# Score bursts in one tile size, another order of loads and other due times in an attention and feed-forward kernel

## The chip, the core and the metric

The kernel runs on one core of a Trainium2 chip. The core has five engines that run their own instruction streams side by side: TensorE (PE in the profile, with its weight loads shown apart as PEld), VectorE (DVE), ScalarE (ACT), GpSimd (POOL) and SyncE (SP). DMA transfers are issued here by POOL, which can convert fp32 to bf16 on the way, and by SP, which also issues the transfers that transpose. The metric is the device time of one execution in microseconds (us); lower is better.

## What is computed

A sliding-window attention with a distance bias, followed by a feed-forward layer with a squared ReLU:

```
q, k, v: [8 batches, 8 heads, 576 positions, 64]      # fp32
scores = (q @ k.T) / 8 + slope[h] * -(|i - j|)         # only for 0 <= i - j < 128
attn   = softmax(scores) @ v
x      = attn as [4608 tokens, 512]
h      = x @ w_in            # [4608, 2048]
out    = max(h, 0)**2 @ w_out  # [4608, 512], fp32
```

## The kernel before

**Blocks.** Each batch's 576 positions are cut into four blocks of 128 and one of 64, so there are 40 blocks, m = 0 to 39, five to a batch. A block's q and k are loaded into one tile of the ring `kq`, its v into one of the ring `vt` (eight and seven tiles; `size`, line 256). They arrive as bf16 through POOL's queue, but for block 0, whose k and q come as fp32 through SP into a tile of their own. A block takes these steps:

- `turn` (429) transposes k and q into a tile `kqT`: blocks 0 to 8 (`KQ_PE`) on PE, with the copies out of PSUM on ACT and DVE (414, 416); the others by a DMA transpose that SP issues (439). After it the `kq` tile is free.
- `score` (501) makes the scores in bursts of matmuls, then takes the exponential on ACT and multiplies by a table of decayed masks on DVE.
- `mix` (593) multiplies by v (609), normalises (632, 637), and transposes x into `xT`: on PE with a DVE copy for the blocks in `X_PE` (655, 414), by a DMA transpose for the others (647).

**Tiles in a burst.** A score matmul contracts over 64 numbers, so two heads lie in the two halves of the rows of the array. From block 6 on (`QUARTERS`) a block that has a left neighbour, and 128 rows, is done in *quarters*: matmuls of 64x64 tiles that leave out the part outside the window (513 to 523, tag `Pq`; L520 in the profile). All others, the *pairs* among them, use 64x128 tiles (524 to 531, tag `P`; L528). A pair is the short last block of a batch with the first of the next: (4,5), (9,10) and so on to (34,35), seven in all. Each block or pair is cut into two units of two head groups; up to pair (4,5) a burst has two units, from block 6 on three (`LONG`, `UNITS`). So a pair from (9,10) on shares bursts with quartered blocks. A pair has 24 matmuls: for each of four head groups, three pieces (64, 64 and 128 columns) in two halves.

**Feed-forward.** The 4,608 tokens form nine groups of 512. `fc_step` (713) makes 16 first-layer tiles a group, each of four matmuls, then ReLU on ACT and the square on DVE; `t_part` (775) sums the second layer over 16 tiles for each 128 tokens, in four parts, each with one quarter of `w_out`. Groups 0 and 1 are split by tokens (`SPLIT`), so that the first tiles need fewer blocks. The weights come in four loads each, i0 to i3 for `w_in` and o0 to o3 for `w_out`. PSUM's eight banks are shared by all of this.

**What sets the order.** Nothing is scheduled by hand. Each piece of work is added to a `Plan` (44) as a task with an engine, a cost in ns, a key, what it waits for and what buffers it takes and frees. `order` (90) simulates the engines: it starts, again and again, the task that can start first, and among those the one with the lowest key. The result is a fixed order of instructions for each engine; on the chip an instruction that has to wait holds up all behind it on its engine. What steers the planner:

- keys. The feed-forward's run from 0, 128 to a group (64 first-layer, 64 second-layer). A block's key is its due time from `where` (418): its last token's number / 4, less 232, less `AHEAD` for the block. Transposes by DMA take due - 80, those of k and q on PE due - 56, scores and masks due - 28, the rest due - 12 to due.
- loads. `FIRST` is the order of the first ten blocks (b) and the weights (i, o) on POOL's queue; they have keys below all others. Later blocks' loads are issued when a tile is free. The planner lets at most eight loads be open in a queue.
- `BEGIN`, POOL's assumed start; `COLD`, the time up to which PE's costs count double; `SHARE, SOON`, which hold back PSUM banks from the feed-forward when a score burst will be ready within `SOON` ns.
- `PAIR_AFTER`: the two DVE copies that build the pairs' masks (316, 319; key -140) wait for this block's masks.
- `WARM` and `FILL`: idle matmuls on a zero tile (815) at the start (four to an instruction), and in holes that the plan shows on PE before `UNTIL`; `fill` (827) puts in so many that they take the share `FILL` of the hole, at 107 ns each before `COLD` and 54 after.

At the end the number of transfers that SP issues is made to fit the eight DMA lanes: `odd` of the stores before the last four go through POOL (753).

Of the kernel before, what the change touches and what calls it, by code (L numbers as in the profile page):

```python
# [38 lines left out]
class Plan:  # L39


    LAT = {"PE": 260.0, "ACT": 220.0, "DVE": 220.0, "POOL": 200.0, "SP": 2200.0}
    BEGIN = {"POOL": 780.0}

    def __init__(self, bufs, pools, cold, share):
        self.tasks = []
# [31 lines left out]
    def order(self):  # L78
# [6 lines left out]
        for t in self.tasks:  # L85
# [3 lines left out]
            for e in t.engs:  # L89
                free.setdefault(e, self.BEGIN.get(e, 800.0))  # L90
                cand.setdefault(e, [])
# [105 lines left out]
def kernel(  # L197
    ctx: ExitStack, tc: tile.TileContext, q, k, v, moe_w_in, moe_w_out, out
):
    nc = tc.nc  # L200
# [10 lines left out]
    C = d_model // 128  # L211
# [1 line left out]
    NG = NT // 512  # L213
    NBLK = B * NKB

    FIRST = "b0 b1 b2 b3 i0 i1 i2 b4 b5 o0 b6 o1 b7 o2 i3 o3 b8 b9"
    SPLIT = {0: [(0, 256), (256, 512)], 1: [(0, 192), (192, 320), (320, 512)]}
    EARLY = 0
    AHEAD = {10: -30, 1: 30, 4: 90, 9: -60, 5: 30, 0: 0, 12: 60, 11: 0, 2: -60, 8: 0, 7: 90, 6: 0, 3: -30, 24: 0, 14: -30, 18: 30, 25: 30, 23: 30, 16: -30, 13: 30, 21: 0, 19: 30, 17: 0, 22: 0, 20: 60, 15: 30}
    LEAD = 40  # L220

    KQ_PE = [0, 1, 2, 3, 4, 5, 6, 7, 8]
    X_PE = [0, 1, 2, 3, 4, 5, 6, 7, 8, 12, 13, 17, 21]
    WARM = 24
    FILL, UNTIL = 0.7, 26e3
    COLD = 8200
    QUARTERS = 6
    V0 = 1
    SHARE, SOON = 3, 1500
    LONG, UNITS = 5, 3  # L230
    W_IN = [0, 4, 8, 12, 16]
    PAIR_AFTER, PAIR_KEY = 1, -140
    BANKS = {"A": 8}
    HOLD, OSB = 12, 14

# [17 lines left out]
        return [const.tile(shape, BF16, name=f"{name}_{i}") for i in range(n)]  # L253


    size = {"kq": 8, "v": 7, "kqT": 5, "P": 2, "x": 4, "Pq": 2, "raw": 2}
    kq = ring("kq", size["kq"], [128, 2, d_model])
    vt = ring("vt", size["v"], [128, H, D + 1])
    kqT = ring("kqT", size["kqT"], [128, 2 * C, 128])
    Pt = {nm: ring(nm, size[nm], [128, H, 2, 128]) for nm in ("P", "Pq")}  # L260
    raw = ring("raw", size["raw"], [128, H, 192])
# [5 lines left out]
    def act(n):  # L267
        return n * 0.84 + 55.0
# [133 lines left out]

    for i, what in enumerate(FIRST.split()):
        {"b": load_block, "i": load_w_in, "o": load_w_out}[what[0]](int(what[1:]), -9e5 + i)
# [13 lines left out]
    def where(m):  # L418
        b, kb = divmod(m, NKB)
        return b, kb, blk[kb], (b * S + kb * 128 + blk[kb]) / 4 - 192 - 40 - AHEAD.get(m, LEAD if m not in X_PE else 0), b == 0  # L420

# [79 lines left out]
    def score(units):  # L501
        first_of = [u for u in units if u[1] == 0]
        due = units[0][0][3]
        slots = {}
        for (ms, sP, work_of, _), j in units:
            for half in range(2):
                slots[ms[0], 2 * j + half] = Slot("A")

        def burst():
            for sl in slots.values():  # L510
                bank(sl)
            for (ms, sP, work_of, _), j in units:
                for c in (2 * j, 2 * j + 1) if sP.tag == "Pq" else ():
                    m = ms[0]
                    for part, k0, q0, q1 in ((1, 0, 0, 128), (1, 64, 64, 128), (0, 64, 0, 128), (0, 0, 0, 64)):
                        mk = m - 1 + part
                        lo = (c % 2) * 256 + at_of[m, part] + q0 - k0
                        for half in range(2):
                            rows = slice(half * 64, half * 64 + 64)
                            nc.tensor.matmul(  # L520
                                slots[m, 2 * j + half].tile[k0:k0 + 64, lo:lo + q1 - q0],
                                kqT[sk_of[mk].idx][rows, c, k0:k0 + 64], kqT[sk_of[m].idx][rows, C + c, q0:q1],
                                start=True, stop=True)
                for c in () if sP.tag == "Pq" else (2 * j, 2 * j + 1):
                    for m, mk, w, at, _ in work_of:
                        for half in range(2):
                            rows = slice(half * 64, half * 64 + 64)
                            nc.tensor.matmul(  # L528
                                slots[ms[0], 2 * j + half].tile.rearrange("p (c x) -> p c x", c=2)[:, c % 2, at:at + w],
                                kqT[sk_of[mk].idx][rows, c, :], kqT[sk_of[m].idx][rows, C + c, 0:w],  # L530
                                start=True, stop=True)
        cost = 220.0 + 2 * sum(88.0 if u[0][1].tag == "Pq" else sum(max(w[2], 64) / 2.4 + 4 for w in u[0][2])
                               for u in units)
        tm = plan.add({"PE": cost}, due - 28, burst,
                      [t for u in units for w in u[0][2] for x in w[:2] for t in t_kq_of[x]] + chain["s"],
                      [*slots.values()] + [u[0][1] for u in first_of if u[0][1].tag == "P"],
                      [x for u in units if u[1] == 1 for w in u[0][2] for x in w[4]])
        tm.n = 4 * sum(4 if u[0][1].tag == "Pq" else len(u[0][2]) for u in units)
        plan.bursts.append(tm)
        chain["s"] = [tm]  # L540
        for (ms, sP, work_of, due), j in units:
            pair = len(ms) == 2
            hi = max(w[3] for w in work_of) // 128 + 1
            lo = min(w[3] for w in work_of) // 128
            n = 128 if pair else work_of[0][2]
            cols = 2 * sum(w[2] for w in work_of)

            def view(t, pair=pair, lo=lo, hi=hi, n=n):
                if pair:
                    return t  # L550
                return t.rearrange("p c (t q) -> p c t q", t=2)[:, :, lo:hi, 0:n]

            for i in (2 * j, 2 * j + 1) if sP.tag == "Pq" else ():
                slot = slots[ms[0], i]
                if i == 0:
                    raw_of[ms[0]] = Slot("raw")
                sr = raw_of[ms[0]]

                def expo(i=i, slot=slot, sr=sr):
                    nc.scalar.activation(raw[sr.idx][:, 2 * i:2 * i + 2],  # L560
                                         slot.tile.rearrange("p (c x) -> p c x", c=2)[:, :, 0:192],
                                         AF.Exp, bias=0.0, scale=scale)
                te = plan.add({"ACT": act(384) + 50.0}, due - 28 + 3 * i, expo, [tm], [sr] if i == 0 else [], [slot])
                for k0 in (0, 64):
                    def mask(i=i, k0=k0, sr=sr, sP=sP):
                        nc.vector.tensor_tensor(  # L566
                            Pt["Pq"][sP.idx].rearrange("p h t q -> p h (t q)")[k0:k0 + 64, 2 * i:2 * i + 2, k0:k0 + 192],
                            raw[sr.idx][k0:k0 + 64, 2 * i:2 * i + 2],
                            masks.rearrange("p h t q -> p h (t q)")[k0:k0 + 64, 2 * i:2 * i + 2, k0:k0 + 192],
                            op=ALU.mult)  # L570
                    P_of[ms[0]][1].append(plan.add(
                        {"DVE": dve(384, 2)}, due - 28 + 3 * i, mask, [te] + t_zero_P + t_mask,
                        [sP] if i == 0 and k0 == 0 else [], [sr] if i == 3 and k0 else []))
            for i in () if sP.tag == "Pq" else (2 * j, 2 * j + 1):
                slot = slots[ms[0], i]

                def Pv(i=i, sP=sP, view=view):
                    return view(Pt["P"][sP.idx][:, 2 * i:2 * i + 2].rearrange("p h t q -> p h (t q)"))

                def expo(i=i, Pv=Pv, view=view, slot=slot):  # L580
                    nc.scalar.activation(Pv(i), view(slot.tile.rearrange("p (c x) -> p c x", c=2)),  # L581
                                         AF.Exp, bias=0.0, scale=scale)
                te = plan.add({"ACT": act(cols) + 50.0}, due - 28 + 3 * i, expo, [tm], [], [slot])

                def mask(i=i, pair=pair, Pv=Pv, view=view):
                    pt = Pv(i)
                    mk = (pair_masks if pair else masks.rearrange("p h t q -> p h (t q)"))[:, 2 * i:2 * i + 2]
                    nc.vector.tensor_tensor(pt, pt, view(mk), op=ALU.mult)  # L588
                P_of[ms[0]][1].append(plan.add(
                    {"DVE": dve(cols, 2)}, due - 28 + 3 * i, mask,  # L590
                    [te] + (t_pair if pair else [t_mask[h] for h in range(H) if place(h) // 2 == i])))
# [73 lines left out]
    sk_of, t_kq_of, parts_of, P_of, at_of = {}, {}, {}, {}, {}  # L665
    m = 0
    raw_of = {}
    units, ready = [], []
    while m < NBLK:
        ms = [m, m + 1] if m % NKB == NKB - 1 and m + 1 < NBLK else [m]  # L670
# [4 lines left out]
        for j in range(2):  # L675
# [6 lines left out]
            units = []  # L682
# [190 lines left out]
```

## Time and profile before

| | us |
|---|---|
| median of 5 runs | 314.63 (313.65 to 315.8) |
| the profiled execution | 315.8 |
| its span in the profile | 314.0 |
| PE busy | 299.0 |
| DVE busy | 184.7 |
| ACT busy | 171.2 |
| POOL busy | 106.1 |
| PE first-layer matmuls (L713) | 148.0 |
| PE second-layer matmuls (L775) | 142.4 |
| first L713 starts | 18.14 |
| last block load issued by POOL | 212.01 |

Times in views of the trace are counted from the start of the span; the rest of the execution's time lies around it. Matmuls follow each other in a pipeline, and the duration of one holds its latency, so durations of neighbours overlap, and a sum of them is more than the time that PE was taken. DMA rows of POOL and SP are the issuing of a transfer, not its landing. A group's line gives the count, the busy time and the mean of one in ns, then the engine's idle time before them.

### The profile page before, as it was taken

How to read it: one execution, taken by the hardware profiler on the slowest of the kernel's cores; microseconds unless marked ns; L12 is line 12 of the kernel's file. 1: busy time of each engine (PE TensorE's matmuls, PEld its weight loads, DVE VectorE, ACT ScalarE, POOL GpSimd, SP SyncE). 2: the span in 40 equal slices, each digit the busy share in tenths (PEclk: the TensorE clock that was granted, in tenths of full speed). 3: DMA queues.
4: the chain of work that ended last, by engine and by line, in shares of the span. 5: the costliest groups of instructions: out<-in, count | busy, mean ns of one | idle time of the engine just before them, and what ended most of it. 6: DMA issues, size and time to landing. Idle time of an engine off the chain costs nothing.

```text
span 314.0 us, 7547 instructions
## 1 busy us (share of the span) xinstructions
PE 299.0 (95%) x2955; PEld 167.9 (53%) x2998; DVE 184.7 (59%) x566; ACT 171.2 (55%) x338; POOL 106.1 (34%) x132
## 2 busy tenths in 40 slices
PE   7879999999989989999999999999999999999996
PEld 3567778767545555554545544554454544444443
DVE  7765677758469597885785853774587522222200
ACT  5867567566166774665665834673564543434411
POOL 8938639565354563474173220000000000000000
PEclk9999999999999999999999999999999999999999
DMA  9999999999999999999999999995312310000022
GB/s 134 150 185 174 189 185 122 141 150 134 134 132 141 155 138 133 145 130 141 128 195 154 203 143 179 257 144 132 111 41 71 111 43 35 33 34 35 33 88 79
DMA packets 167668, 39.76 MB, mean 127 GB/s; under 512 B 158864, under 2 KB 163216, under 8 KB 167632
## 3 DMA queue, kind: packets, MB, share of 16 engines
q0 software_dynamic: 114736, 18.36, 84.8%
q1 hardware_dynamic: 52896, 20.92, 41.3%
q8 instruction: 23, 0.38, 0.5%
q14 instruction: 13, 0.11, 0.1%
HBM read 36.70 MB, written 9.44 MB: 147 GB/s over the span
## 4 chain that ended last, share of the span: by engine, by line
PE 81%; DMA 8%; DVE 4%; POOL 4%; issue 2%; ACT 1%; POOLq 0%
PE A L713 36%; PE A L775 35%; PE A L609 5%; DMA kqT<-kq 4%; DMA kq<-in_q_dram 4%; PE A L520 3%; DVE Pq L566 2%; POOL kq L397 2%; PE A L528 1%; POOL vt L397 1%; PE A L655 1%; ACT raw L560 1%; PE A L467 1%; DVE x L637 1%; POOL w_in_sb L366 1%
## 5 line engine op out<-in xcount | busy, mean ns | idle before, releaser
L713 PE MATMUL A<-xT,w_in_sb 128*128 128x512 bf16 (+3 forms) x757 | 148.0, 325 | 3.1 <-DMA w_in_sb<-in_moe_w_in_dram 2.0
L775 PE MATMUL A<-w_out_sb,g 128*128 128x512 bf16 (+2 forms) x560 | 142.4, 373 | 2.6 <-issue 1.9
L722 ACT ACTIVATE rt<-A 128x512 bf16<-128x512 f32 (+1 forms) x148 | 86.5, 591 | 99.8 <-PE A L713 76.6
L729 DVE TENSOR_TENSOR g<-rt 128x512 bf16<-128x512 bf16 (+1 forms) x148 | 60.7, 412 | 75.0 <-ACT rt L722 74.2
L713 PEld LDWEIGHTS <-w_in_sb 128*128 128x128 bf16 x768 | 68.5, 98 | 53.4 <-DMA w_in_sb<-in_moe_w_in_dram 2.6
L775 PEld LDWEIGHTS <-g 128*128 128x128 bf16 x592 | 54.0, 98 | 54.3
L566 DVE TENSOR_TENSOR Pq<-raw,masks 64x384 bf16<-64x384 bf16 x168 | 59.1, 352 | 9.7 <-ACT raw L560 6.3
L397 POOL DMA_DIRECT2D vt<-in_v_dram x40 | 34.1, 854 | 53.6 <-PE A L609 33.7
L397 POOL DMA_DIRECT2D kq<-in_k_dram x39 | 33.6, 861 | 33.8 <-DMA kqT<-kq 17.1
L397 POOL DMA_DIRECT2D kq<-in_q_dram x39 | 33.5, 859 | 16.4 <-DMA kq<-in_q_dram 6.2
L560 ACT ACTIVATE raw<-A 128x384 bf16<-128x384 f32 x84 | 35.7, 501 | 4.3 <-PE A L520 3.8
L745 ACT ACTIVATE osb<-A 128x512 f32<-128x512 f32 (+1 forms) x36 | 21.5, 598 | 22.7 <-PE A L775 22.4
L637 DVE TENSOR_TENSOR x<-A,rec 128x256 bf16<-128x256 f32 (+1 forms) x80 | 31.8, 412 | 0.7
L753 POOL DMA_DIRECT2D out_dram<-osb x1 | 0.6, 587 | 85.5 <-ACT osb L745 85.5
L581 ACT ACTIVATE P<-A 128x512 bf16<-128x512 f32 (+1 forms) x48 | 23.7, 577 | 4.2 <-PE A L528 4.1
L632 DVE RECIPROCAL rec<-A 128x4 f32<-128x4 f32 (+1 forms) x80 | 12.8, 173 | 14.2 <-PE A L609 13.3
L609 PEld LDWEIGHTS <-Pq 128*128 128x128 bf16 x336 | 15.6, 97 | 10.0 <-DVE Pq L566 1.2
L609 PE MATMUL A<-vt,Pq 128*128 128x65 bf16 x336 | 17.4, 193 | 1.6 <-DVE x L637 0.9
L588 DVE TENSOR_TENSOR P<-P,pair_masks 128x512 bf16<-128x512 bf16 x28 | 11.6, 421 | 3.4 <-ACT P L581 2.6
L609 PEld LDWEIGHTS <-P 128*128 128x128 bf16 x240 | 10.8, 98 | 4.8
L609 PE MATMUL A<-vt,P 128*128 128x65 bf16 x240 | 11.8, 193 | 0.0
L520 PEld LDWEIGHTS <-kqT 64*64 64x64 bf16 x672 | 8.4, 108 | 6.0 <-issue 5.7
(43 smaller groups left out, 109.2 us busy)
## 6 DMA issues: line engine op xcount, KB each, us to landing
out_dram<-osb SPq DMA_DIRECT2D x34, 256.0 KB, 2.3
vt<-in_v_dram POOLq DMA_DIRECT2D x32, 128.0 KB, 10.2
kq<-in_k_dram POOLq DMA_DIRECT2D x31, 128.0 KB, 11.2
kq<-in_q_dram POOLq DMA_DIRECT2D x31, 128.0 KB, 11.0
w_in_sb<-in_moe_w_in_dram POOLq DMA_DIRECT2D x4, 512.0 KB, 11.6
w_out_sb<-in_moe_w_out_dram POOLq DMA_DIRECT2D x4, 512.0 KB, 9.9
kq<-in_k_dram POOLq DMA_DIRECT2D x8, 64.0 KB, 12.4
kq<-in_q_dram POOLq DMA_DIRECT2D x8, 64.0 KB, 12.2
```

What stands on the lines that cost most here:

```text
L397: nc.gpsimd.dma_start(o, src[b, :, kb * 128:kb * 128 + n, :].rearrange("h s d -> s h d"))
L520: nc.tensor.matmul(slots[m, 2 * j + half].tile[k0:k0 + 64, lo:lo + q1 - q0], kqT[sk_of[mk].idx][rows, c, k0:k0 + 64], kqT[sk_of[m].idx][ro ...
L560: nc.scalar.activation(raw[sr.idx][:, 2 * i:2 * i + 2], slot.tile.rearrange("p (c x) -> p c x", c=2)[:, :, 0:192], AF.Exp, bias=0.0, scale ...
L566: nc.vector.tensor_tensor(Pt["Pq"][sP.idx].rearrange("p h t q -> p h (t q)")[k0:k0 + 64, 2 * i:2 * i + 2, k0:k0 + 192], raw[sr.idx][k0:k0 ...
L581: nc.scalar.activation(Pv(i), view(slot.tile.rearrange("p (c x) -> p c x", c=2)), AF.Exp, bias=0.0, scale=scale)
L609: nc.tensor.matmul(bank(slot_v)[:, hi * (D + 1):(hi + 1) * (D + 1)], Pt[sP.tag][sP.idx][:, place(h)].rearrange("p t q -> p (t q)")[:, at_o ...
L637: nc.vector.tensor_tensor(xt[sx.idx][0:n, hf * 256:(hf + 1) * 256].rearrange("p (h e) -> p h e", h=4), pv[0:n, :, 0:D], srec.tile[0:n, :]. ...
L713: nc.tensor.matmul(bank(slot)[:, fi * w:(fi + 1) * w], w_in_sb[:, cc, fc * 128:(fc + 1) * 128], xT[:, cc, g * 512 + lo:g * 512 + hi], star ...
L722: nc.scalar.activation(srt.tile[:, 0:cols], slot.tile[:, 0:cols], AF.Relu, bias=0.0, scale=1.0)
L729: nc.vector.tensor_tensor(sg.tile[:, fcs[0]:fcs[-1] + 1, lo:hi], r, r, op=ALU.mult)
L745: nc.scalar.activation(so.tile[:, lo:hi], slot.tile[:, lo:hi], AF.Copy)
L775: nc.tensor.matmul(bank(slot)[:, lo:hi], sg.tile[:, fc, t * 128:(t + 1) * 128], w_out_sb[:, fc, lo:hi], start=fc == 0, stop=fc == FCB - 1)
```

## The change

In `score`, a burst that holds a quartered unit makes its other units with 64x64 tiles too: each of their matmuls, 128 columns of the array wide, becomes two of 64, one for each half of the keys. The columns that stream through are the same. Bursts without a quartered unit are as before.

In `FIRST` the quarters of the weights move: o0 ahead of b4, i3 and o1 ahead of b6, o2 behind b7, o3 between b8 and b9. In `AHEAD` six blocks get another value: 4 from 90 to 60, 5 from 30 to 60, 8 from 0 to -30, 3 from -30 to 30, 14 from -30 to 60, 13 from 30 to 90. Blocks 13 and 21 leave `X_PE`, so their x is transposed by DMA. The ring `kq` has seven tiles for eight. Five numbers of the planner and of the fillers change, and the pairs' masks are built after block 2 instead of block 1.

```diff
--- before.py
+++ after.py
@@ -40,7 +40,7 @@
 
 
     LAT = {"PE": 260.0, "ACT": 220.0, "DVE": 220.0, "POOL": 200.0, "SP": 2200.0}
-    BEGIN = {"POOL": 780.0}
+    BEGIN = {"POOL": 1260.0}
 
     def __init__(self, bufs, pools, cold, share):
         self.tasks = []
@@ -213,23 +213,23 @@
     NG = NT // 512
     NBLK = B * NKB
 
-    FIRST = "b0 b1 b2 b3 i0 i1 i2 b4 b5 o0 b6 o1 b7 o2 i3 o3 b8 b9"
+    FIRST = "b0 b1 b2 b3 i0 i1 i2 o0 b4 b5 i3 o1 b6 b7 o2 b8 o3 b9"
     SPLIT = {0: [(0, 256), (256, 512)], 1: [(0, 192), (192, 320), (320, 512)]}
     EARLY = 0
-    AHEAD = {10: -30, 1: 30, 4: 90, 9: -60, 5: 30, 0: 0, 12: 60, 11: 0, 2: -60, 8: 0, 7: 90, 6: 0, 3: -30, 24: 0, 14: -30, 18: 30, 25: 30, 23: 30, 16: -30, 13: 30, 21: 0, 19: 30, 17: 0, 22: 0, 20: 60, 15: 30}
+    AHEAD = {10: -30, 1: 30, 4: 60, 9: -60, 5: 60, 0: 0, 12: 60, 11: 0, 2: -60, 8: -30, 7: 90, 6: 0, 3: 30, 24: 0, 14: 60, 18: 30, 25: 30, 23: 30, 16: -30, 13: 90, 21: 0, 19: 30, 17: 0, 22: 0, 20: 60, 15: 30}
     LEAD = 40
 
     KQ_PE = [0, 1, 2, 3, 4, 5, 6, 7, 8]
-    X_PE = [0, 1, 2, 3, 4, 5, 6, 7, 8, 12, 13, 17, 21]
-    WARM = 24
-    FILL, UNTIL = 0.7, 26e3
-    COLD = 8200
+    X_PE = [0, 1, 2, 3, 4, 5, 6, 7, 8, 12, 17]
+    WARM = 28
+    FILL, UNTIL = 0.4, 26e3
+    COLD = 12000
     QUARTERS = 6
     V0 = 1
-    SHARE, SOON = 3, 1500
+    SHARE, SOON = 3, 500
     LONG, UNITS = 5, 3
     W_IN = [0, 4, 8, 12, 16]
-    PAIR_AFTER, PAIR_KEY = 1, -140
+    PAIR_AFTER, PAIR_KEY = 2, -140
     BANKS = {"A": 8}
     HOLD, OSB = 12, 14
 
@@ -253,7 +253,7 @@
         return [const.tile(shape, BF16, name=f"{name}_{i}") for i in range(n)]
 
 
-    size = {"kq": 8, "v": 7, "kqT": 5, "P": 2, "x": 4, "Pq": 2, "raw": 2}
+    size = {"kq": 7, "v": 7, "kqT": 5, "P": 2, "x": 4, "Pq": 2, "raw": 2}
     kq = ring("kq", size["kq"], [128, 2, d_model])
     vt = ring("vt", size["v"], [128, H, D + 1])
     kqT = ring("kqT", size["kqT"], [128, 2 * C, 128])
@@ -501,6 +501,7 @@
     def score(units):
         first_of = [u for u in units if u[1] == 0]
         due = units[0][0][3]
+        tall = 64 if any(u[0][1].tag == "Pq" for u in units) else 128
         slots = {}
         for (ms, sP, work_of, _), j in units:
             for half in range(2):
@@ -523,19 +524,21 @@
                                 start=True, stop=True)
                 for c in () if sP.tag == "Pq" else (2 * j, 2 * j + 1):
                     for m, mk, w, at, _ in work_of:
-                        for half in range(2):
-                            rows = slice(half * 64, half * 64 + 64)
-                            nc.tensor.matmul(
-                                slots[ms[0], 2 * j + half].tile.rearrange("p (c x) -> p c x", c=2)[:, c % 2, at:at + w],
-                                kqT[sk_of[mk].idx][rows, c, :], kqT[sk_of[m].idx][rows, C + c, 0:w],
-                                start=True, stop=True)
+                        for k0 in range(0, 128, tall):
+                            for half in range(2):
+                                rows = slice(half * 64, half * 64 + 64)
+                                nc.tensor.matmul(
+                                    slots[ms[0], 2 * j + half].tile.rearrange("p (c x) -> p c x", c=2)[
+                                        k0:k0 + tall, c % 2, at:at + w],
+                                    kqT[sk_of[mk].idx][rows, c, k0:k0 + tall], kqT[sk_of[m].idx][rows, C + c, 0:w],
+                                    start=True, stop=True)
         cost = 220.0 + 2 * sum(88.0 if u[0][1].tag == "Pq" else sum(max(w[2], 64) / 2.4 + 4 for w in u[0][2])
                                for u in units)
         tm = plan.add({"PE": cost}, due - 28, burst,
                       [t for u in units for w in u[0][2] for x in w[:2] for t in t_kq_of[x]] + chain["s"],
                       [*slots.values()] + [u[0][1] for u in first_of if u[0][1].tag == "P"],
                       [x for u in units if u[1] == 1 for w in u[0][2] for x in w[4]])
-        tm.n = 4 * sum(4 if u[0][1].tag == "Pq" else len(u[0][2]) for u in units)
+        tm.n = 4 * sum(4 if u[0][1].tag == "Pq" else len(u[0][2]) * 128 // tall for u in units)
         plan.bursts.append(tm)
         chain["s"] = [tm]
         for (ms, sP, work_of, due), j in units:
```

## The prediction

> **What bounds the kernel now.** I read the busy shares first, then the time by stage, then the rows in which TensorE (PE) stands still, each with what ended the wait.
>
> ```profile
> PE 299.0 (95%) x2955; PEld 167.9 (53%) x2998; DVE 184.7 (59%) x566; ACT 171.2 (55%) x338; POOL 106.1 (34%) x132
> ...
> 0.00:18.00 18.00, 13.93 (x154) 8.35 (x154) 13.19 (x48) 12.63 (x29) 15.49 (x23) 1.00 1.58 146
> 18.00:30.00 12.00, 10.17 (x135) 8.37 (x136) 7.00 (x22) 7.17 (x15) 7.12 (x9) 1.00 1.84 181
> ...
> 240.00:300.00 60.00, 59.63 (x314) 27.84 (x320) 17.57 (x48) 26.11 (x46) 0.59 (x1) 1.00 0.15 50
> ```
>
> The columns of a stage are its length, then the busy time of PE, PE's weight loads, DVE, ACT and POOL. From 30 us on PE hardly rests, so a matmul saved there is time saved, and PE executes in a fixed order, so one late operand holds everything behind it. Up to 18 us PE is busy too, but with little of use: the first feed-forward matmul starts at 18.14, released by the first `w_in` load. Column counts at the pace of the rows (a 512-column matmul each 0.215 us) put the useful work up to there at about 6 us. So 12 us go at the start, some 6 in stalls and switches between 18 and 120, and 2.9 at the end after the last matmuls. The stalls on PE that count:
>
> ```profile
> 18.14 1.27 PE L713 MATMUL A<-xT,w_in_sb 128*128 128x256 bf16 x10 [0.57 <-DMA w_in_sb<-in_moe_w_in_dram]
> ...
> 21.73 0.39 PE L713 MATMUL A<-xT,w_in_sb 128*128 128x256 bf16 x2 [1.44 <-DMA w_in_sb<-in_moe_w_in_dram]
> ...
> 87.65 0.23 PE L528 MATMUL A<-kqT 64*128 64x128 bf16 x2 [0.88 <-DMA kqT<-kq]
> ...
> 114.60 0.40 PE L609 MATMUL A<-vt,Pq 128*128 128x65 bf16 x8 [0.94 <-DVE x L637]
> ```
>
> In brackets stands the idle time before the row and what ended it. Together these four are 3.8 us: the most that better orders can win after 18 us.
>
> **The 64x64 tiles.** Six of the seven pairs share a burst with 64x64-tiled blocks; pair (4,5) has its own. There 24 matmuls of 64x128 become 48 of 64x64, 144 more in all. The rows of weight loads show the two kinds in one burst:
>
> ```profile
> 92.18 0.26 PEld L528 LDWEIGHTS <-kqT 64*128 64x128 bf16 x12 [0.42 <-issue]
> 92.52 0.41 PEld L520 LDWEIGHTS <-kqT 64*64 64x64 bf16 x32
> 73.88 0.58 PEld L520 LDWEIGHTS <-kqT 64*64 64x64 bf16 x48 [0.16 <-issue]
> ```
>
> Gain: the first kind ends at 92.44, the second starts at 92.52; against the regular step of some 0.02 us this switch costs about 0.06. A pair is cut into two units, and eight bursts hold both kinds: 8 x 0.06 = 0.5 us. Cost: 48 small loads take 0.58 us, the last alone 0.107, so one each 10 ns, with matmul starts 11.4 ns apart (0.54 us for 48). A pair would take 48 x 11.4 = 0.55 us where now 24 take 0.49 (0.48 to 0.49 us of loads): +0.06, times 6 = +0.35. Net **-0.1 us**. Ends: -0.5 if the pairs cost no more, and +2.1 if the four quadrants didn't overlap and a pair's 0.43 us of columns doubled (6 x 0.43 = 2.6, less 0.5). The rows with 48 starts in 0.54 us exclude most of that, since their columns one after another would be 1.9 us.
>
> Two rules of the Trainium skill stand here, both on the page TensorEngine Tiling (Array Packing). "Key Properties" says that a change of tiling mode drains the array: for the change, and the row prices it at 0.06, not at a full matmul's latency of 0.2. "Instruction Overhead" speaks against it: every matmul has about 60 cycles of overhead, 25 ns at 2.4 GHz, so that 48 small ones would take 1.2 us for 0.49 and six pairs lose 4.3 us. The row has them 11.4 ns apart with four tiles at work, so I take +0.35.
>
> **Two blocks fewer turned on PE (13 and 21).** Removes 8 transposes of 128 columns, 53 ns each, 0.43 us, and the stall of 0.16 in front of block 13's at 93.22. I take **-0.5 us**. Two DVE evacuations (0.42 us each) go too, beside PE. SP gets two more DMA transposes of 1.2 us each. Behind them in SP's queue stand kqT transposes, whose scores come 20 us or more later, except around 87. Landing takes 7.2 us (2.3 to 10.5). Block 21 was ready at 134.8 and its group is next, so at worst a wait of some 2 us there; the lead of SP makes me take 0. The count for the DMA lanes sends three stores instead of one through POOL, which is otherwise idle at the end: 0.
>
> **Order of the loads.** Blocks 0 to 3 and i0 to i2 stay first, so the start at 18.14 stays. POOL's stalls date the landings behind them: a load waits for the eighth before it, and o0, block 6's k and o2 issue at 21.98, 24.52 and 30.92, at once after i1, i2 and o0 landed. From 24.5 to 30.9 block 4 (half a block), block 5 and o0 came: 2.1 MB, so 3.0 us for a weight load and 2.3 for a block. Re-adding in the new order: o0 3.4 us earlier, blocks 4 and 5 3 later, i3 10 earlier, block 6 6 later, o1 1 later, block 7 and o2 3 later, block 8 3 earlier, o3 2 later. What PE has meanwhile: first-layer work with i0 to i2 (10.2 us), with i3 3.4, each w_out quarter 3.4. From 18.1 with i0 to i2 alone it is fed to 29.8, with o0 to 33, with i3 (34) and o1 (37) past 40. So the later blocks are covered, if the order puts that work first.
>
> **Start-up.** PAIR_AFTER 2 moves two DVE copies (0.61 and 0.55 us at 12.5 to 13.8) behind block 2's masks; block 3, with due -134 for -74, has mask keys of -162, ahead of the copies' -140. FILL 0.4 and COLD 12000 thin the fillers: one of 1.19 us at 14.98 stood in front of the transposes of blocks 0 and 1 and of block 3's scores. Both bring block 3's x, ready at 26 and needed for the second half of group 0, nearer to the hole of 1.44 us before 21.73. I take half of it: **-0.7 us**, ends 0 and -1.4. WARM 28 is one idle matmul more in time spent waiting for block 0; BEGIN and SOON touch only the plan. Against fewer fillers stands the skill's TensorE: Matmul & The Clock Gate (Part 1, the HAM clock gate): PE idle for a window of about 3.4 us halves its clock, which would cost some 1.7 us at 18. The trace grants 1.00 in every stage, and around the 1.44 hole PE was busy 2.06 of 3.5 us without slowing. I take 0.
>
> **Seven k and q tiles.** Block 0 takes no tile, so block m waits for the turning of m-7 instead of m-8. The first load that this holds back is block 19 (issued at 71.7, the tile that it takes is block 12's, turned between 62 and 75 by the six SP transposes from 50.7 to 72.0 and their 9.5 us of landing), used at 112. Later leads are longer. Behind a waiting k stand v loads, but planned order can pass them. Fewer early k and q loads mean less traffic beside the kqT transposes, among them the one of 12.7 us (from 74.9) that ended the 0.88 wait. Due times move blocks 13 and 14 up. The waits of 0.88 and 0.94 are places where a fixed order met a late operand; either may go or be replaced. I take half of 1.8: **-0.9 us**.
>
> **Sum.** -0.1 - 0.5 - 0.7 - 0.9 = -2.2 us. The profiled execution took 315.8 (span 314.0 and 1.8 around it), so 313.6 by its own time; it was 1.2 above the median of 314.63, which gives **312.4**. What is late next is x of group 2: by 94.05 PE had loaded 127 of the 128 weights for the second layer of groups 0 and 1, so it then needs group 2:
>
> ```profile
> L775 PEld LDWEIGHTS <-g 128*128 128x128 bf16 x127 | 11.5, 98 | 9.2
> ```
>
> Block 11's x went to DMA at 82.53; with 7.2 to 10.5 us it lands at 89.7 to 93.0. So PE may come 1.1 to 4.4 us earlier, and the 0.7 + 0.9 fits.
>
> **Rivals.**
> *No change.* Landing takes 10.5 us, PE waits at 94 for what was won before, and a new stall replaces 114.6: only the 0.5 is left: 314.1. For it: the 127 of 128, and no slack is visible. Against it: the median landing.
> *Slower.* The plan believes in earlier loads than come: adding its own costs, i2 lands at 21.1, and it landed at 24.3. PE's transposes of blocks 4 to 6 may be placed where the plan has them, 3 us early, with weight work behind them. A hole of the size of the old one (1.44) before each of the three is +4.3, less the 0.5 and 0.1: 318.3. It decides once such a transpose stands in front of second-layer work whose weights are there. For it: this is what made the hole at 20.3, and block 6 comes 6 us later. Against it: 10 to 17 us of first-group work wait in that stretch.
> *The tiles don't merge.* If the 60-cycle rule held: -2.2 + 4 = 316.4. The rows contradict it.
>
> **Chances.** My forecast 0.47, no change 0.25, slower by the late blocks 0.24, by the tiles 0.04. A measurement can tell about 0.5%, 1.6 us, from no change: faster below 313.1, slower above 316.2. So 0.47 faster, 0.25 same, 0.28 slower. The forecast's own range is 310.0 (all four parts at their good end: -0.5, -0.6, -1.4, -1.8, with a little of the 0.57) to 313.6; the range that holds 8 in 10 goes on to 318.0.
>
> **What would show it.** No 64*128 rows beside 64*64 ones after 60 us, and 48 loads in about 0.58 us in every burst of three; 44 transposes of x on PE instead of 52; a wait under 0.8 us before the second weight quarter; first-layer work of group 2 before 93. Wrong: a wait of over 1 us at L467 between 25 and 45, PE idle near 93, or a granted clock under 1.00.

## The result, and the profile after

| | before | after |
|---|---|---|
| median, us | 314.57 (79 runs) | 313.34 (42 runs) |
| ratio, 95% interval | | 0.9961 [0.9949, 0.9973] |
| the profiled execution, its span | 315.8, 314.0 | 312.08, 310.3 |

The changed kernel is faster by 0.4%, 1.2 us. That is clear of zero, but inside the 0.5% that the prediction had set as the least to tell from no change (faster below 313.1). Two later comparisons of the same kernel gave 0.9983 [0.9965, 1.0001] and 0.9934 [0.9918, 0.9950]; weighted by the inverse squares of the intervals the three give 0.996. The two profiled executions lie 3.7 us apart, three times as much as the medians: one came from the upper part of its kernel's spread (312.9 to 317.7), the other from the lower end of its own (312.0 to 316.4). What one trace says of a wait that depends on a load has to be read with that in mind.

The busy shares and granted clock of the changed kernel, then its time by stage (length, busy time of PE, PE's weight loads, DVE, ACT and POOL, then the clock):

```profile
PE 297.9 (96%) x3080; PEld 168.9 (54%) x3123; DVE 184.1 (59%) x563; ACT 171.8 (55%) x339; POOL 107.3 (35%) x134
...
PEclk9589999999999999999999999999999999999999
...
0.00:18.00 18.00, 14.25 (x125) 9.03 (x127) 11.32 (x42) 11.79 (x27) 15.56 (x24) 0.72 1.59 153
18.00:30.00 12.00, 11.73 (x147) 10.17 (x143) 8.73 (x28) 7.84 (x16) 6.62 (x8) 0.99 1.62 189
240.00:300.00 60.00, 59.69 (x315) 27.89 (x320) 16.05 (x43) 24.65 (x44) 1.69 (x3) 1.00 0.14 49
```

Two things stand out. PE is busy for 11.73 of 12 us from 18 to 30, where it was 10.17; much of that is chance, since in the two later profiles of the same kernel it is 11.95 and 10.90, and with the old start and the tiles alone 11.48. And the clock of PE, which was full everywhere, is at half from 8 to 18 us. These are the rows of PE that answer to the four stalls shown of before:

```profile
18.43 0.83 PE L716 MATMUL A<-xT,w_in_sb 128*128 128x256 bf16 x6
...
25.58 1.24 PE L778 MATMUL A<-w_out_sb,g 128*128 128x512 bf16 x4 [0.21 <-DMA w_out_sb<-in_moe_w_out_dram]
...
85.34 2.32 PE L778 MATMUL A<-w_out_sb,g 128*128 128x512 bf16 x10 [0.16 <-issue]
...
111.46 0.40 PE L612 MATMUL A<-vt,Pq 128*128 128x65 bf16 x8 [1.01 <-DVE x L640]
```

In this execution the waits for `w_in` and for the transposed k and q tile are gone, the second weight quarter is waited for 0.21 us, and the wait for x on DVE is still there, 1.01 for 0.94. The bursts, shown by their weight loads:

```profile
89.37 0.29 PEld L530 LDWEIGHTS <-kqT 64*64 64x64 bf16 x24 [0.42 <-issue]
89.58 0.44 PEld L521 LDWEIGHTS <-kqT 64*64 64x64 bf16 x32
```

The same burst began at 92.18 and ended at 92.93 before, 0.75 us; now it ends at 90.02, after 0.65. The second line begins at 89.58 while the last load of the first is still going until 89.66: without a switch the two kinds overlap by 0.08, where before there was a gap of 0.08.

### The profile page after: what moved, and what is told of

Its sections match the earlier page's. It is cut to its first block, busy times and chain, and to the rows that moved or that the text cites. A ratio compares the mean times of both kernels' runs of the same rounds, so it can differ in the third digit from the quotient of the medians.

```text
span 310.3 us, 7797 instructions
## 1 busy us (share of the span) xinstructions
PE 297.9 (96%) x3080; PEld 168.9 (54%) x3123; DVE 184.1 (59%) x563; ACT 171.8 (55%) x339; POOL 107.3 (35%) x134
## 4 chain that ended last, share of the span: by engine, by line
PE 84%; DVE 4%; DMA 4%; POOL 4%; issue 2%; ACT 1%; POOLq 0%; ACTq 0%
PE A L716 38%; PE A L778 36%; PE A L612 5%; DMA w_out_sb<-in_moe_w_out_dram 4%; DVE Pq L569 3%; PE A L521 3%; POOL kq L397 2%; PE A L530 1%; POOL vt L397 1%; ACT raw L563 1%; POOL w_in_sb L366 1%; PE A L467 1%; DVE x L640 0%; PE A L658 0%; DVE P L591 0%
## 5 line engine op out<-in xcount | busy, mean ns | idle before, releaser
L756 POOL DMA_DIRECT2D out_dram<-osb x3 | 1.7, 562 | 84.4 <-ACT osb L748 84.4
L612 PEld LDWEIGHTS <-P 128*128 128x128 bf16 x240 | 11.8, 102 | 4.3
L612 PE MATMUL A<-vt,P 128*128 128x65 bf16 x240 | 12.9, 199 | 0.2 <-DVE x L640 0.2
```

The source lines that it names most:

```text
L612: nc.tensor.matmul(bank(slot_v)[:, hi * (D + 1):(hi + 1) * (D + 1)], Pt[sP.tag][sP.idx][:, place(h)].rearrange("p t q -> p (t q)")[:, at_o ...
```

## The experiments

Each was timed in five rounds beside the kernel before. Ratios are to it, with the 95% interval; the interval is some 0.2% (0.6 us) to each side, so what a part is worth is read from the traces where it can be. One measure from the traces needs no luck: the time from PE's 449th load of `w_in` weights (group 4's first) to its last load of `g`, which is the stretch from 145 us to the end. Nothing waits there for long, and it repeats to 0.05 us. The same can be taken from the 321st load (group 2's first) or the 385th (group 3's), where the two kernels have the same work left or the difference can be counted.

### The tiles alone

```diff
 # the kernel before, with score() of the changed one
+        tall = 64 if any(u[0][1].tag == "Pq" for u in units) else 128
```

> The kernel before with the 64x64 tiles alone; every engine keeps its order, PE gets 144 small matmuls more. My prediction's term: -0.1 us (six pairs at +0.06, eight switches saved at 0.06), so a ratio of 0.9997. The changed kernel's trace speaks for more: its mixed bursts take 0.71, 0.65 and 0.72 us where before they took 0.79, 0.75 and 0.78, some 0.08 less in each of eight: -0.6 us, 0.998. By the rule of 60 cycles a matmul: +4 us, 1.013. The rows of the 64x64 loads tell: 48 in about 0.53 for a pair, and no gap between the two kinds.

Measured: 0.9985 [0.9967, 1.0004], 313.89 us to 314.31. The interval leaves out the loss by the 60 cycles, and can't tell -0.1 from -0.6. The traces can. Whole bursts of before, from the first load to the end of the last, against the same ones here: 0.80 and 0.70 (147.6), 0.73 and 0.65 (170.0), 0.75 and 0.64 (175.3). And the stretch from the 449th load to the end takes 165.94 us before and 165.59 here, 0.35 for the four mixed bursts in it: **0.09 in each**. The four bursts before that stretch are shorter by as much (0.07 to 0.09), so 0.7 us over eight is the most. Not all of it arrives: from group 2's first load to the end, with five bursts in it, the gain is 0.36 (217.02 to 216.66), for behind the burst at 112.7 PE waits for x on DVE, 0.94 us before and 1.01 here. All kernels below with the tiles take 165.58 to 165.62 there, all without 165.93 to 165.97.

This trace also shows how much of the start is luck, since up to 64 us every engine has the instructions of before, in the same order:

```profile
18.02 1.27 PE L716 MATMUL A<-xT,w_in_sb 128*128 128x256 bf16 x10 [0.52 <-DMA w_in_sb<-in_moe_w_in_dram]
...
20.52 0.39 PE L716 MATMUL A<-xT,w_in_sb 128*128 128x256 bf16 x2 [0.34 <-DMA w_in_sb<-in_moe_w_in_dram]
...
66.15 0.24 PE L521 MATMUL A<-kqT 64*64 64x128 bf16 x4 [0.96 <-DMA kqT<-kq]
```

The hole of 1.44 us is one of 0.34; and the wait of 0.88 at 87.65 is not there, while one of 0.96 stands at 66.15.

### The start and the due times alone

```diff
-    FIRST = "b0 b1 b2 b3 i0 i1 i2 b4 b5 o0 b6 o1 b7 o2 i3 o3 b8 b9"
+    FIRST = "b0 b1 b2 b3 i0 i1 i2 o0 b4 b5 i3 o1 b6 b7 o2 b8 o3 b9"
 # with the new AHEAD, BEGIN, WARM, FILL, COLD, SOON, PAIR_AFTER; X_PE, kq and score() as before
```

> The kernel before with the new order of loads, due times, start-up numbers, fillers and pair masks, and without the tiles, the seven k and q tiles, and the two blocks moved to DMA. If the gain comes from the start, as I hold, this has nearly all of it: first-layer work from 18.4 us on without the wait of 1.44 us, ratio 0.996 (-1.2 us) or lower. If the gain comes from tiles, transposes and fewer k and q tiles instead, the start gives nothing: 0.999 to 1.001. If the parts belong together (the plan is re-made as a whole), it may be slower than before: over 1.002.

Measured: 0.9974 [0.9952, 0.9995]. The wait before the second `w_in` quarter is gone, but there are waits of 0.21 for the third, 0.77 for o0 and, at 118.15, 1.16 us for x that a DMA turned. By its ratio the start gains 0.8 us; beside the tiles and the transposes such a gain is not found again (below).

### The fillers of before in the changed kernel

```diff
-                    n = int((t.start - at) * FILL / (107.0 if t.start < COLD else 54.0))
+                    n = int((t.start - at) * 0.7 / (107.0 if t.start < 8200 else 54.0))
```

> The changed kernel with as many fillers as before (share 0.7, the 107 ns price up to 8.2 us only); all other instructions and their order are as in the changed kernel. The changed kernel's trace shows a granted clock of 0.50 from 8 to 18 us, which I had taken to stay at 1.00. If the halved clock costs what it could (3 us of work at half speed, with the first FFN matmuls behind it), the granted clock is back at 1.00 here and the ratio to before falls by 0.003 or more below the changed kernel's 0.996. If the work up to 18 us waits for loads anyway, the clock is back and the time is the same, 0.996 within 0.001. If fillers stand in the way of real work, it is slower, 0.998 or more.

Measured: 0.9977 [0.9954, 1.0001]. The stages from 8 us:

```profile
8.00:18.00 10.00, 6.20 (x111) 4.26 (x110) 6.65 (x22) 8.18 (x20) 8.64 (x12) 1.00 1.74 154
18.00:30.00 12.00, 10.89 (x111) 9.07 (x113) 6.30 (x22) 6.32 (x13) 5.59 (x7) 0.86 1.64 188
```

The clock is full up to 18, and then fell for part of the next stage, after a hole of 2.30 us before the first weights at 19.06. The edit brings back only part of the fillers: up to the first weights they are 3.41 us of columns at full clock, for 2.29 in the changed kernel and 4.96 before (the holes that the rule fills are others in this plan). Of twelve runs eight kept a granted clock of 1.00, with a median of 313.16, and four lost some, at 314.02. With 2.29 us, 38 of 43 runs of the changed kernel lose some, with a median of 313.35, against 312.85 for the five that don't; with 4.96, the kernel before lost none in 35 runs beside these. So the lower clock that I had priced at nothing by expecting it not to come does come, and the more often the fewer the fillers are, though before has another order too. By the medians it goes with 0.5 to 0.9 us, with few runs on one side; two profiles of the changed kernel below give a better price, 0.1 at most and 0.7. More fillers did not make this kernel faster: 0.9977 stands beside 0.9973 for the next one, which has the few fillers.

### Eight k and q tiles in the changed kernel

```diff
-    size = {"kq": 7, "v": 7, ...
+    size = {"kq": 8, "v": 7, ...
```

> The changed kernel with eight k and q tiles again. The plan is re-made from the eighth block's load on. My prediction gave the seven tiles a part in the two stalls of 0.88 and 0.94 us (half of 1.8): with eight, the wait for a transpose near 85 is back and the ratio to before is 0.998 to 0.999. If seven tiles do nothing (the first load held back is used 40 us later), it stays at 0.996. If seven tiles cost time, it goes under 0.994.

Measured: 0.9973 [0.9954, 0.9992], and a profile of 312.51 without the wait near 85. The wait does not come back, and the first group-2 load comes at 91.42, within the 91.0 to 92.7 of the changed kernel. Seven or eight makes no difference that can be seen here.

### Tiles and transposes, without the start and the seven tiles

```diff
 # the kernel before, with score() of the changed one, and
-    X_PE = [0, 1, 2, 3, 4, 5, 6, 7, 8, 12, 13, 17, 21]
+    X_PE = [0, 1, 2, 3, 4, 5, 6, 7, 8, 12, 17]
```

> The kernel before with the 64x64 tiles and with blocks 13 and 21 turned by DMA; start, due times, order of loads and eight k and q tiles as before. Theory A, now: tiles (0.08 us in each of eight bursts) and transposes (0.43) are the whole gain of 1.2 us, and the start's holes were the luck of one execution: ratio 0.9964, as the changed kernel, and from the first matmul of group 2 to the end 0.8 us less than before. Theory B, my prediction: the start brings over half, so only 0.6 of 1.2 us is here, 0.998.

> The kernel before with the tiles and the two transposes by DMA, once more, for a narrower number. Theory A (tiles and transposes are the gain): the same ratio as the changed kernel beside it, within 0.0015, around 0.9965. Theory B (the start is half of it): 0.0015 or more above the changed kernel.

Measured: 0.9974 [0.9950, 0.9997] and, in a second job, 0.9960 [0.9936, 0.9985]: some 1.0 us, most of the 1.2. From group 2's first load on I expected 0.8 us less than before; it takes 217.29, for 217.02. But this plan has loaded 124 second-layer weights by then where before had 127, so three matmuls of 0.215 us more stand in the stretch, and PE waits 0.40 us more in it (waits of over 0.15 us: 2.92 for 2.52). These two take up 1.05 us, so the work itself is shorter by about 0.8. The start that it shares with before gave two more draws of the hole before the second quarter, 1.11 us and 0.40. These are the rows of the second:

```profile
18.18 1.27 PE L716 MATMUL A<-xT,w_in_sb 128*128 128x256 bf16 x10 [0.72 <-DMA w_in_sb<-in_moe_w_in_dram]
20.73 0.39 PE L716 MATMUL A<-xT,w_in_sb 128*128 128x256 bf16 x2 [0.40 <-DMA w_in_sb<-in_moe_w_in_dram]
23.81 0.72 PE L716 MATMUL A<-xT,w_in_sb 128*128 128x256 bf16 x5 [0.45 <-DMA w_in_sb<-in_moe_w_in_dram]
```

### The changed kernel again

> The changed kernel once more, beside the others on one chip. Ratio 0.9961 as measured. Its profile is a second look at the start: if the gap of 3.7 us between the two profiled executions was luck of loads, the first group-2 matmul comes later than 91.0 us here, at 91.5 to 92.5.

> The changed kernel once more, for the same comparison: 0.9961 was measured at first, 0.9983 the second time; around 0.997 here. Its trace is a third look at the start: first-layer matmuls from 18.1 to 18.9 us on, with at most 0.3 us of waits for weights behind it, and one wait of about 1 us near 86 for a transposed k and q tile or none.

Measured: 0.9983 [0.9965, 1.0001] with the two-part kernel at 0.9974 beside it, and 0.9934 [0.9918, 0.9950], on six runs, with 0.9960 beside it. One time the whole change is 0.0009 behind its two parts, the other time 0.0026 ahead. By the line that I had drawn at 0.0015 the second speaks for theory B, that the start is half of the gain, and the first for A. With 0.003 to each side neither decides; over both jobs what is left for start, due times and seven tiles is about 0.3 us, less than this can resolve. The wait near 86 came in the first (0.98) and not in the second. Group 2 begins at 92.7 us in the first (expected 91.5 to 92.5), so the 3.7 us between the two first profiles are in large part luck.

In the second the first weights came earlier than I expected, and PE waited for weights for 0.67, 0.67 and 0.29 us, where I had expected at most 0.3:

```profile
17.14 0.83 PE L716 MATMUL A<-xT,w_in_sb 128*128 128x256 bf16 x6 [0.67 <-DMA w_in_sb<-in_moe_w_in_dram]
20.22 1.05 PE L716 MATMUL A<-xT,w_in_sb 128*128 128x256 bf16 x8 [0.67 <-DMA w_in_sb<-in_moe_w_in_dram]
25.47 1.24 PE L778 MATMUL A<-w_out_sb,g 128*128 128x512 bf16 x4 [0.29 <-DMA w_out_sb<-in_moe_w_out_dram]
```

The three profiles of the changed kernel have one order of instructions and three different clocks. The stage from 8 to 18 us of the first profile, of the second and of the third:

```profile
8.00:18.00 10.00, 8.99 (x101) 6.48 (x102) 5.70 (x20) 7.73 (x18) 8.71 (x13) 0.50 1.82 172
8.00:18.00 10.00, 6.89 (x95) 5.10 (x96) 5.36 (x19) 7.45 (x18) 9.06 (x13) 0.75 1.81 170
8.00:18.00 10.00, 7.37 (x122) 5.39 (x122) 7.26 (x23) 8.44 (x20) 9.26 (x13) 1.00 1.81 173
```

The first quarter of `w_in` lands at 17.64, 17.30 and 17.09 us. At full clock PE is there before it and waits. At half clock it is late: it comes to its first `w_in` matmul at 18.43 and, in the second profile, at 18.91, which is 0.8 and 1.6 us after the landing:

```profile
18.91 1.28 PE L716 MATMUL A<-xT,w_in_sb 128*128 128x256 bf16 x6
```

That is why these two have no wait before the second quarter, which lands at 20.13 and 20.23. Most of the delay is made up while the third profile waits for weights. At the 257th `w_in` load the three stand at 60.66, 61.22 and 60.55. The first is 0.1 behind the third, no more than o0 landed later in it (25.54 for 25.43), so its lost clock cost nothing that can be seen; in the second it cost 0.7.

### The changed kernel without tiles and transposes

```diff
 # the changed kernel, with score() of the one before, and
-    X_PE = [0, 1, 2, 3, 4, 5, 6, 7, 8, 12, 17]
+    X_PE = [0, 1, 2, 3, 4, 5, 6, 7, 8, 12, 13, 17, 21]
```

> The changed kernel without the tiles and with blocks 13 and 21 turned on PE: start, order of loads, due times and seven k and q tiles alone. Theory A: nothing left, 0.999 to 1.001. Theory B: 0.998 or less. The run of the start without the seven tiles gave 0.9974 with an interval of 0.002 to each side, so A allows 0.9985 at the least. From the first matmul of group 2 to the end it must take what before took, 217.0 us, by both.

Measured: 1.0052 [1.0023, 1.0081]: slower than before, which neither theory had. The stretch from group 2's first matmul takes 218.6 us for 217.0, with one long wait in it. PE's row, then SP's rows (issue time, time in SP) of this kernel:

```profile
118.11 1.24 PE L713 MATMUL A<-xT,w_in_sb 128*128 128x512 bf16 x5 [2.75 <-DMA xT<-x]
```

```profile
100.16 2.57 SPq L647 DMA_TRANSPOSE xT<-x  x2
102.97 2.82 SPq L439 DMA_TRANSPOSE kqT<-kq  x1
110.08 1.19 SPq L647 DMA_TRANSPOSE xT<-x  x1
```

Group 3 needs the x of block 16. It is issued at 110.08, and the x transposes of this stretch take 6.8 to 8.8 us to land; PE comes earlier and waits 2.75 us. In the changed kernel the third one goes with the other two:

```profile
90.22 1.19 SPq L650 DMA_TRANSPOSE xT<-x  x1
91.58 8.32 SPq L439 DMA_TRANSPOSE kqT<-kq  x3
99.95 5.57 SPq L650 DMA_TRANSPOSE xT<-x  x3
```

So the third is out by 105.5, and no PE row waits for it. The row at 90.22 is block 13's x, on DMA now. With it the planner made another order, in which block 16 is done sooner. The tiles leave the order as it is, so it is the moved blocks that take away a wait that the new start would run into; in this company they are worth more than the 0.43 us of their transposes.

### Two more blocks turned by DMA

```diff
-    X_PE = [0, 1, 2, 3, 4, 5, 6, 7, 8, 12, 17]
+    X_PE = [0, 1, 2, 3, 4, 5, 6, 7, 8]
```

> The changed kernel with blocks 12 and 17 turned by DMA too; none but blocks 0 to 8 are turned on PE. If a transpose on PE costs its 0.21 us wherever x comes in time, another 0.43 us goes: 0.9947. Block 12 is needed for group 2 at 91 us, when PE has run out of second-layer work, and was ready at 82: if landing takes 8 to 10 us there, it just holds; if not, PE waits at 91 and the gain is lost or more, 0.997 to 1.002. Block 17 was ready at 119.1 and used at 119.7, with about 38 second-layer matmuls (8 us) left to do.

Measured: 1.0009 [0.9992, 1.0026], beside 0.9983 for the changed kernel. Group 2 did hold: no wait stands before its first matmul, and the one of 0.16 us just ahead of it is in the changed kernel too. Group 3 did not:

```profile
118.91 7.07 PE L716 MATMUL A<-xT,w_in_sb 128*128 128x512 bf16 x32 [1.39 <-DMA xT<-x]
```

The wait uses up what was saved. From group 2's first load to the end this kernel takes 216.16 us, for 216.19 in the changed kernel: four transposes and one second-layer matmul fewer, and the wait of 1.39 us in place of the one of 1.01 for x on DVE. So turning these two by DMA gains nothing from there on; why the ratio is 0.8 us worse, with 0.8 to each side, that stretch doesn't show.

### Seven k and q tiles alone

```diff
 # the kernel before, with
-    size = {"kq": 8, "v": 7, ...
+    size = {"kq": 7, "v": 7, ...
```

> The kernel before with seven k and q tiles alone. My prediction: they take traffic away beside the transposes and help, with the due times, to remove a stall: 0.998 to 1.000. Rival: they only re-make the plan. In the run of the start with seven tiles and 13 and 21 on PE, PE waited 2.75 us at 118 for x turned by DMA, and with eight 1.2 us, so seven without the two moved blocks may cost 1 to 2 us: 1.003 to 1.006. In both, from 145 us on it takes what before takes, 165.9 us.

Measured: 0.9970 [0.9954, 0.9987], although its trace has a wait of 1.34 us for a transposed k and q tile at 85.75. That is 0.9 us faster, more than I had expected of them, and the trace doesn't show by what. With the other parts they don't help (the run with eight). It is the new start with seven tiles and without the moved blocks that hurts. Taken alone, tiles, start and seven k and q tiles gain 0.5, 0.8 and 0.9 us by their ratios, which is more than the whole change does.

### Normalising first

```diff
-            t1 = plan.add({"DVE": 97.0}, due - 12 + 4 * hf, rec, [last], [srec])
+            t1 = plan.add({"DVE": 97.0}, due - 12 + 4 * hf - 200, rec, [last], [srec])
 # and the same key for norm
```

> The changed kernel with the reciprocal and the normalisation on DVE given a key 200 lower, so that they go ahead of masks of later blocks. The wait of 1.01 us at 113 (PE for x on DVE, behind nine masks of 0.35) is the one that every kernel so far had. If it goes and nothing comes in its place: 1.0 us less than the changed kernel, 0.994. If the masks are late instead, PE waits for Pq: the same as the changed kernel, or up to 1 us slower.

Measured: 1.0006 [0.9988, 1.0025], 1 us and more slower than the changed kernel. The wait at 113 is gone, and there are others for it, one of them, the first here, for a load of weights:

```profile
26.45 0.81 PE L779 MATMUL A<-w_out_sb,g 128*128 128x512 bf16 x2 [1.17 <-DMA w_out_sb<-in_moe_w_out_dram]
...
77.80 0.84 PE L613 MATMUL A<-vt,Pq 128*128 128x65 bf16 x22 [0.52 <-DVE Pq L570]
82.58 0.25 PE L531 MATMUL A<-kqT 64*64 64x128 bf16 x4 [0.59 <-DMA kqT<-kq]
```

The masks are later, as the second case had it; the wait at 26 can be luck of the loads. No version beat the changed kernel by more than the noise.

## Why the prediction was right, and where its sum was not

The direction and the range held: 313.34 in 310.0 to 318.0. The forecast itself was 2.2 us of gain, and 1.2 came, which lies in what the prediction itself called the same, a case to which it gave 0.25. Three of the four terms of the sum were mis-sized: the tiles were put far too low, and the start and the stalls, 1.6 of the 2.2 us, were taken from draws of one execution. That the direction came out right is in part luck, as the first error made up for much of the other two.

What the traces show without luck is the stretch from group 2's first load to the last `g` load: 217.02 us before, 216.19 in all three profiles of the changed kernel. Of these 0.83 us the tiles are 0.36 and block 21's transposes 0.23; the other 0.24 are what eight matmuls of the attention take that the new order has already done by then, so no gain. Ahead of group 2 stand three more mixed bursts and block 13's transposes, by the same prices some 0.5 us if no wait takes them up. Together that is 1.1 of the 1.2 us, an estimate, which leaves little for start and stalls.

**The tiles, -0.1.** Each of the eight bursts is shorter by 0.09, 0.7 us at the most, and 0.36 of 0.44 arrives from group 2 on. The cost was right: 48 loads take 0.53 to 0.57 us for 0.49. The gain of a saved switch was not 0.06. I took the gap between the end of one kind's loads and the start of the next, less a step; but loads of one kind overlap, so a switch costs the gap *and* the lost overlap. From the start of the last load of one kind to the start of the next kind's first it is 0.172 us before, and 0.022 in the changed kernel: 0.15 for a switch. The loss by 60 cycles a matmul did not come, as the row had said.

**Blocks 13 and 21 off PE, -0.5.** For block 21 the traces show it. From group 3's first load on, the tiles alone take 190.83 us and the changed kernel 190.60 in all its profiles, with the same loads in that stretch but for the four transposes: 0.23 for the 0.21 of the rows. Block 13's lie ahead of group 2, where the draws hide them. The ratios agree: the tiles alone are at -0.5 us, with the transposes at -0.8 and -1.2. What I had not counted is what the move does to the plan: without it the new start waits 2.75 us for block 16.

**The start, -0.7.** It was half of a hole of 1.44 us, which is one draw. Five executions with the old start have 1.44, 0.34, 1.11, 0.40 and 0.39 us before the second quarter, as the load lands, 0.74 on average. Three profiles of the changed kernel have 0, 0 and 0.67, but in the two with none PE came late, at half clock; the one at full clock also waits 0.67 before the first quarter. So the order of loads and due times was not shown to shrink the hole. The landings behind it did move, by at least the 3.4 and 10 us of the re-adding: o0 lands at 25.4 to 25.5 us for 29.4 to 30.9, and i3 at 31.6 to 31.9 for 42.1 to 43.6. What PE gains by them is not shown. The kernel with the old start and the two other parts is within 0.3 us of the changed one over both jobs. The start alone at -0.8 us speaks for more; that was not settled.

**The stalls, -0.9.** I took half of 0.88 and 0.94. The change does not take away the wait for x on DVE: it is 1.01 us in every profile of the changed kernel. With the start alone it is gone, but one of 1.16 stands at 118 for it. The wait for a transposed tile is luck again: gone with the old plan in the tiles' run, back with 0.98 in one profile of the changed kernel, absent from two. Seven tiles don't decide it.

**What was late next.** Group 2's x was not: at 91.1 the changed kernel had loaded the same 127 of 128 weights as before at 94.05, 2.9 us earlier, and no wait stood there. That moment is 92.7 and 91.2 in the other two profiles, again without a wait. The pinch was one group later, at 118, for x turned by DMA, and only in kernels other than the changed one.

**The clock.** I took 0 for it, and named a granted clock under 1.00 as a sign of being wrong. The sign came, in 38 of 43 runs. I had weighed an idle window of about 3.4 us, and there was none: before the clock fell at 7.9 us PE's longest idle time was 1.58. PE was busy for 1.67 of the 3.42 us before the fall. Its row with that idle time, and the stretch up to the fall:

```profile
6.47 0.66 PE L449 MATMUL A<-ident,kq 128*128 128x128 f32 x4 [1.58 <-DMA kq<-in_q_dram]
```

```profile
4.50:7.92 3.42, 1.67 (x18) 1.19 (x16) 2.50 (x7) 2.70 (x9) 3.42 (x5) 1.00 2.13 137
```

The time was mostly not lost, 0.1 us at most in one profile and 0.7 in another, as PE at full clock waits for weights there.

**The rivals.** The slower case, transposes of blocks 4 to 6 in front of work that was ready, did not happen: no wait of 0.15 us or more at the k and q transposes (L467) between 25 and 45. The case of no change, 314.1, was a little nearer to the result than the forecast of 312.4. Its reason held in part: the stall at 114.6 stayed, as one of 1.01 us, but no wait stood before group 2, and more was left than the 0.5 of the transposes.

## What to carry to other kernels

Before a stall in a profile is put into a sum, find out whether it is in the plan or in that execution: a wait for a load at a place where all loads are queued is a draw, and half of a draw is no estimate. A change between kinds of tiles in one burst costs the overlap of the weight loads besides the gap that the rows show, so take it from start to start. When PE no longer waits for a load, look whether the load came sooner or PE later. In a kernel whose order a planner makes, parts of a change don't add: test the whole beside its parts, and look at what the new order makes late.

## What the runs showed of the hardware

A switch between 64x128 and 64x64 tiles in a burst costs 0.15 us (0.172 from load to load, for 0.022 without it).

The first quarter of `w_in`, the eleventh transfer in POOL's queue, landed at 17.64, 17.30 and 17.09 us in three profiles of the changed kernel. With the same ten transfers ahead of it, it landed at 19.01 in the run with more fillers.

The granted clock of PE fell to 0.50 from 7.9 to 18.2 us in one profile of the changed kernel and from 13.0 to 19.9 in another, and stayed at 1.00 in the third, with the same instructions in the same order. By columns, useful work and fillers fill about 43% of the time up to the first weights there (7.85 of 18.43 us). In the kernel before it is about 59% (10.73 of 18.14), and it kept 1.00 in all of its 35 runs beside the first experiments, and lost some in one of 29 beside the last. At which share the clock falls, these runs don't show. The trace counts a slow matmul as longer busy (a score matmul of 128 columns 0.32 us for 0.22), so a busy share measured after the fall says little of what led to it.
